# Seven half-block products in place of eight in a linear-attention and gated feed-forward kernel

## The chip, the cores and the metric

The kernel runs on one core of a Trainium2 chip. The metric is the time of one execution in microseconds (us), the median over several runs. A core has five engines, each with its own queue of instructions that it takes in order: TensorE (PE, matrix products into PSUM), VectorE (DVE), ScalarE (ACT), GpSimd (POOL) and SyncE (SP, which here only issues DMAs; POOL and ACT issue some too). PE's weight loads are shown apart, as PEld. An engine that needs another's result waits at that instruction, and all that is queued behind it waits too.

## The reference

Batch 8, 8 heads, 576 positions, head width 64; 4608 tokens of width 512; hidden width 1024.

```python
phi = lambda x: np.where(x > 0, x, np.exp(x) - 1.0) + 1.0
kv  = einsum('bhsd,bhse->bhde', phi(k), v);  z = sum(phi(k), axis=2)
num = einsum('bhsd,bhde->bhse', phi(q), kv)
den = einsum('bhsd,bhd->bhs', phi(q), z)[..., None] + 1e-06
x   = (num / den), as 4608 rows of 512
out = ((x @ w1) * (x @ w2)) @ w3 @ w_out
```

Inputs and output are float32; matrix products take bfloat16.

## The kernel before

The 576 positions of a batch are cut into 512 "main" rows (four tiles of 128) and a tail of 64. Two batches give nine tiles of 128 tokens (four, four, and one of both tails), and all 36 tiles are nine chunks of 512 tokens. The program has five kinds of work:

- The folded output weight (`w3_tr`, `wf_mm`): w3 is transposed on PE and multiplied with w_out, so that only one product follows the gates.
- phi (`phi_exp`, `phi_min`, `phi_max`): ACT takes exp to bfloat16; DVE takes min(exp, 1) in place, and then max(x + 1, that) head by head in one instruction of 256 elements with the float32 input (L162).
- Attention: `kv_half` makes phi(k)^T v with a column of ones beside v (so that z comes along), from the two 64-row halves of PE, added by ACT and DVE. A transpose DMA (`qt_load`) or PE (`q_tr`) turns phi(q). `nat_units` multiplies it with kv in half-height products of 65 columns for one or two tiles and divides on DVE: add, reciprocal, product (L271 to L275). `xt_load` or `xt_tr` turns the result to `xt`, channels by tokens. Batch 0 goes by its own path (`first_kvz`, `first_nd`).
- Gates (`f_unit`): for each of eight blocks of 128 hidden columns, four products of 512 columns for a (w1) and four for b (w2); ACT copies a out of PSUM (L376), DVE multiplies it with b to bfloat16 `ab` (L377).
- Output (`o_unit`, `o_store`): eight products of 512 columns for each tile of tokens, one eviction (L393), one store.

The order is written by hand in the string `ORDER`: each word is one unit, and the engines' queues are filled in the order of the words. A letter names the unit, the first number the batch or chunk, and a plus another engine for the copy or the queue. `GATES` holds some loads back until others have landed. What decides besides is the number of buffers: PSUM has four banks of `mm` for gates and output and two buffers of two banks, `at`, for attention; SBUF has five buffers for loaded halves and wholes of q, k and v (`ld`).

```python
def f_unit(c, f):
    a_ps, b_ps = f_open(c, f)
    for ps, w in ((a_ps, w1_sb), (b_ps, w2_sb)):
        for kc in range(KC):
            f_mm(c, f, ps, w, kc)
    f_close(c, f, a_ps, b_ps)
```

Of the kernel before, what the change touches and what calls it, by code (L numbers as in the profile page):

```python
# [14 lines left out]
NCH = 512  # L15


@with_exitstack
def kernel(
# [14 lines left out]
    NTOK = B * S  # L34
# [7 lines left out]
    n_chunks = NTOK // NCH  # L42

    tile_of, order = {}, []
    for b in range(0, B, 2):
        for key in [("J", b, j) for j in range(NJ)] + [("J", b + 1, j) for j in range(NJ)] + [("R", b, 0)]:
            tile_of[key] = len(order)
            order.append(key)  # L50
        tile_of["R", b + 1, 0] = tile_of["R", b, 0]
    NT = len(order)
# [3 lines left out]
    ld = ctx.enter_context(tc.tile_pool(name="ld", bufs=5))  # L56
    ldr = ctx.enter_context(tc.tile_pool(name="ldr", bufs=8))
    setup = ctx.enter_context(tc.tile_pool(name="setup", bufs=2))
# [3 lines left out]
    lr = ctx.enter_context(tc.tile_pool(name="lr", bufs=2))  # L62
    ab_p = ctx.enter_context(tc.tile_pool(name="ab", bufs=2))
    sm = ctx.enter_context(tc.tile_pool(name="sm", bufs=3))
    mm_ps = ctx.enter_context(tc.tile_pool(name="mm_ps", bufs=4, space=bass.MemoryType.PSUM))
    at_ps = ctx.enter_context(tc.tile_pool(name="at_ps", bufs=2, space=bass.MemoryType.PSUM))


    ident = consts.tile([P, P], BF16)
    mask = consts.tile([P, 2, 2, D], BF16)  # L70
    eps = consts.tile([P, 1], F32)
    zero = consts.tile([P, NCH], BF16)

    w1_sb = wpool.tile([P, KC, DFF], BF16)
    w2_sb = wpool.tile([P, KC, DFF], BF16)
    wo_sb = wpool.tile([P, FC, DM], BF16)
    wf_sb = wpool.tile([P, FC, DM], BF16)
    xt = wpool.tile([P, NT, KC, P], BF16)
    vt = wpool.tile([P, NJ, H, D + 1], BF16)
    vr = wpool.tile([P, H // 2, D + 1], BF16)  # L80

    def constants(part):
        if part == 0:
            make_identity(nc, ident)
        elif part == 1:

            nc.gpsimd.memset(mask, 0.0)
            nc.gpsimd.memset(mask[0:D, :, 0, :], 1.0)
            nc.gpsimd.memset(mask[D:P, :, 1, :], 1.0)
            nc.gpsimd.memset(eps, 1e-6)  # L90
            nc.gpsimd.memset(vt[:, :, :, D:D + 1], 1.0)
            nc.gpsimd.memset(vr[:, :, D:D + 1], 1.0)
        else:
            nc.vector.memset(zero, 0.0)

    def warm_up(n):

        ps = mm_ps.tile([P, NCH], F32, tag="mm", name="warm")
        for _ in range(n):
            nc.tensor.matmul(ps, zero[:, 0:P], zero, start=True, stop=True)  # L100


    raw = {}

    def load_qkv(name, src, b, part, alt=False):


        if part == 3:
            t = raw[name + "r", b] = ldr.tile([P, RW], F32, tag="ldr", name=f"{name}32r")
            for hh in range(2):  # L110
                (nc.gpsimd if alt else nc.sync).dma_start(  # L111
                    out=t[hh * R:(hh + 1) * R].rearrange("p (h d) -> p h d", d=D),
                    in_=src[b, hh * 4:(hh + 1) * 4, NJ * P:S, :].rearrange("h p d -> p h d"))
            return None
        if (name, b) not in raw:
            raw[name, b] = ld.tile([P, JW], F32, tag="ld", name=f"{name}32")
        t = raw[name, b]
        h0, h1 = ((0, 4), (4, 8), (0, 8))[part]
        W = NJ * D
        return nc.sync.dma_start(  # L120
            out=t[:, h0 * W:h1 * W].rearrange("p (h x) -> p h x", x=W),
            in_=src[b, h0:h1, 0:NJ * P, :].rearrange("h (p j) d -> p h (j d)", j=NJ))


    ph = {}

    es = {}

    def phi_exp(name, b, g):

        if g == 2:
            x, e = raw[name + "r", b], e_p.tile([P, RW], BF16, tag="er", name="er")
        else:
            x = raw[name, b][:, g * (JW // 2):(g + 1) * (JW // 2)]
            e = e_p.tile([P, JW // 2], BF16, tag="e", name="e", bufs=4)
        es[name, b, g] = x, e
        nc.scalar.activation(out=e, in_=x, func=AF.Exp)  # L137

    def phi_min(name, b, g):
        e = es[name, b, g][1]  # L140
        nc.vector.tensor_scalar_min(out=e, in0=e, scalar1=1.0)  # L141

    def phi_max(name, b, hp):

        if (name, b) not in ph:
            ph[name, b] = [None, None]
        if hp == KC:
            dr = ph[name, b][1] = phi_p.tile([P, RW], BF16, tag=name + "r", name=name + "r", bufs=3)
            todo = [(dr, *es[name, b, 2])]
        else:  # L150
            if hp == 0:
                ph[name, b][0] = phi_p.tile([P, KC, NJ, 2, D], BF16, tag=name + "j", name=name + "j")
            dj = ph[name, b][0]
            x, e = es[name, b, hp // 2]
            W = NJ * D
            todo = []
            for u in range(2):
                h = 2 * (hp % 2) + u
                todo.append((dj[:, hp, :, u, :], *(t[:, h * W:(h + 1) * W].rearrange(
                    "p (j d) -> p j d", d=D) for t in (x, e))))  # L160
        for out, x, e in todo:
            nc.vector.scalar_tensor_tensor(  # L162
                out=out, in0=x, scalar=1.0, in1=e, op0=ALU.add, op1=ALU.max)

    def copy_of(alt):
        return nc.vector.tensor_copy if alt else nc.scalar.copy

    def v_unit(b, i, alt=False):

        if i < 2:  # L170
            copy_of(alt)(  # L171
                out=vt[:, :, 4 * i:4 * i + 4, 0:D],
                in_=raw["v", b].rearrange("p (h j d) -> p j h d", h=H, j=NJ)[
                    :, :, 4 * i:4 * i + 4])
        else:
            copy_of(alt)(out=vr[:, :, 0:D], in_=raw["vr", b].rearrange("p (h d) -> p h d", d=D))


    kvs, qts, xns = {}, {}, {}

    def kv_half(b, g):


        kj, kr = ph["k", b]
        if g == 0:
            kvs[b] = att.tile([P, KC, 2, D + 1], BF16, tag="kv", name="kv")
        kvp = at_ps.tile([P, 2, 512], F32, tag="at", name="kvp")
        W = 2 * (D + 1)
        for i in range(2):
            hp = 2 * g + i  # L190
            steps = [(kj[:, hp, j].rearrange("p u d -> p (u d)"),
                      vt[:, j, 2 * hp:2 * hp + 2, :].rearrange("p h e -> p (h e)"), (0, 1))
                     for j in range(NJ)]
            steps.append((kr[:, i * P:(i + 1) * P],
                          vr[:, 2 * i:2 * i + 2, :].rearrange("p h e -> p (h e)"), (g,)))
            for n, (kk, vv, halves) in enumerate(steps):
                for r in halves:
                    rows = slice(r * R, (r + 1) * R)
                    nc.tensor.matmul(  # L199
                        kvp[:, r, i * W:(i + 1) * W], kk[rows], vv[rows],  # L200
                        start=(n == 0), stop=(n == (NJ if r == g else NJ - 1)))
        kvf = lr.tile([P, 2 * W], F32, tag="kvf", name="kvf")
        nc.scalar.copy(out=kvf, in_=kvp[:, 0, 0:2 * W])  # L203
        nc.vector.tensor_tensor(
            out=kvs[b][:, 2 * g:2 * g + 2].rearrange("p a u e -> p (a u e)"), in0=kvf,
            in1=kvp[:, 1, 0:2 * W], op=ALU.add)

    def kv_full(b, g):

        kj, kr = ph["k", b]  # L210
        if g == 0:
            kvs[b] = att.tile([P, KC, 2, D + 1], BF16, tag="kv", name="kv")
        kvp = at_ps.tile([P, 2, 512], F32, tag="at", name="kvp")
        W = 2 * (D + 1)
        rows = slice(g * R, (g + 1) * R)
        for i in range(2):
            hp = 2 * g + i
            for j in range(NJ):
                nc.tensor.matmul(kvp[:, 0, i * W:(i + 1) * W],
                                 kj[:, hp, j].rearrange("p u d -> p (u d)"),  # L220
                                 vt[:, j, 2 * hp:2 * hp + 2, :].rearrange("p h e -> p (h e)"),
                                 start=(j == 0), stop=False)
            nc.tensor.matmul(kvp[:, 0, i * W:(i + 1) * W], kr[rows, i * P:(i + 1) * P],
                             vr[rows, 2 * i:2 * i + 2, :].rearrange("p h e -> p (h e)"),
                             start=False, stop=True)
        return kvp[:, 0, 0:2 * W]

    def kv_copy(b, g, p, alt=False):
        copy_of(alt)(out=kvs[b][:, 2 * g:2 * g + 2].rearrange("p a u e -> p (a u e)"), in_=p)

# [400 lines left out]
```

## Time and profile before

| | us |
|---|---|
| median of three runs (260.99 to 262.19) | 261.28 |
| span of the profiled execution | 258.1 |
| PE busy | 237.4 |
| DVE busy | 167.9 |
| ACT busy | 129.0 |
| POOL busy | 21.1 |
| PE, gate products a and b (L371) | 75.1 and 74.9 |
| PE, output products (L390) | 63.2 |
| ACT, waits of the copy of a (L376) for PE | 55.6 |

The profile is of one execution. Busy time is the union of an engine's instructions, so that two that overlap count once. Matmuls overlap: each has a duration of 380 ns at 512 columns, but the next starts earlier. The span runs from the first to the last instruction; the rest of a run's time lies around it. A group's line in the profile names the source line, the engine, the tiles, shapes and types, how often it occurs, then its busy time and the mean duration, then the idle time before it and what ended that.

### The profile page before, as it was taken

What the parts mean: (1) busy time and instruction counts of PE and PEld (TensorE: products, weight loads), DVE (VectorE), ACT (ScalarE), POOL (GpSimd) and SP (SyncE); (2) the same over time, 40 slices, a digit from 0 to 9 for tenths busy, and PEclk for the clock granted to TensorE, in tenths of its full rate; (3) what the DMA queues carried; (4) which work ended last, traced back from release to release, by engine and by line L of the source; (5) the groups of instructions that cost most, each with busy time, mean ns of one, the idle gap of its engine ahead of it and who ended that gap; (6) DMA issues with size and microseconds to landing.
All of it is one profiled execution on the core that took longest, in us unless ns stands there. A gap on an engine that the chain in (4) does not pass through costs nothing.

```text
span 258.1 us, 4507 instructions
## 1 busy us (share of the span) xinstructions
PE 237.4 (92%) x1656; PEld 116.2 (45%) x1673; DVE 167.9 (65%) x426; ACT 129.0 (50%) x205; POOL 21.1 (8%) x42
## 2 busy tenths in 40 slices
PE   1138999999999999999999999999999999999994
PEld 1124554545454454455444444444444444444442
DVE  0025787969978979997968589468866543423320
ACT  2048587858478664677353645726533203331421
POOL 8000765000101000000000000000000000000000
PEclk9999999999999999999999999999999999999999
DMA  6999999999898599939988975934980124003024
GB/s 100 200 257 378 316 229 245 208 334 307 302 291 250 87 340 215 307 104 253 211 193 245 369 160 123 248 99 131 218 220 26 34 57 124 0 37 125 3 82 163
DMA packets 70085, 48.98 MB, mean 190 GB/s; under 512 B 34416, under 2 KB 64368, under 8 KB 70064
## 3 DMA queue, kind: packets, MB, share of 16 engines
q1 hardware_dynamic: 63104, 42.54, 61.4%
q0 software_dynamic: 6816, 6.03, 14.1%
q8 instruction: 13, 0.21, 0.3%
q10 hardware_dynamic: 144, 0.13, 0.1%
q14 instruction: 8, 0.07, 0.1%
HBM read 38.80 MB, written 9.44 MB: 187 GB/s over the span
## 4 chain that ended last, share of the span: by engine, by line
PE 84%; DMA 8%; ACT 2%; SPq 1%; issue 1%; DVE 1%; DVEq 0%; POOLq 0%
PE a_ps L371 25%; PE b_ps L371 24%; PE o_ps L390 23%; DMA k<-in_k_dram 4%; DMA w3b<-in_moe_w_dram 4%; PE kvp L199 3%; PE wf_ps L464 3%; PE nd L265 3%; SPq L111 1%; PE tp L309 1%; PE w3p L454 1%; PE xtp L285 1%; PE o_ps L417 1%; DVE qj L162 1%; ACT e L137 0%
## 5 line engine op out<-in xcount | busy, mean ns | idle before, releaser
L371 PEld LDWEIGHTS <-w_sb 128*128 128x128 bf16 x576 | 54.2, 98 | 63.4 <-issue 0.5
L377 DVE TENSOR_TENSOR ab<-a_sb,b_ps 128x512 bf16<-128x512 f32 x72 | 49.0, 684 | 46.6 <-PE b_ps L371 35.4
L371 PE MATMUL a_ps<-xt,w_sb 128*128 128x512 bf16 x288 | 75.1, 380 | 0.1
L371 PE MATMUL b_ps<-xt,w_sb 128*128 128x512 bf16 x288 | 74.9, 379 | 0.0
L376 ACT COPY a_sb<-a_ps 128x512 f32<-128x512 f32 x72 | 41.9, 586 | 56.8 <-PE a_ps L371 55.6
L390 PE MATMUL o_ps<-wf_sb,ab 128*128 128x512 bf16 x266 | 63.2, 379 | 0.7
L390 PEld LDWEIGHTS <-ab 128*128 128x128 bf16 x280 | 26.7, 98 | 30.8
L393 ACT COPY o_sb<-o_ps 128x512 f32<-128x512 f32 x24 | 14.0, 583 | 30.7 <-PE o_ps L390 30.7
L162 DVE SCALAR_TENSOR_TENSOR kj<-k,e 128x256 bf16<-128x256 f32 x64 | 23.6, 417 | 0.1
L162 DVE SCALAR_TENSOR_TENSOR qj<-q,e 128x256 bf16<-128x256 f32 x64 | 23.4, 417 | 0.1
L141 DVE TENSOR_SCALAR e<-e 128x1024 bf16<-128x1024 bf16 x32 | 13.4, 420 | 14.2 <-ACT e L137 14.2
L137 ACT ACTIVATE e<-q 128x1024 bf16<-128x1024 f32 x16 | 16.7, 1058 | 9.3 <-DMA q<-in_q_dram 9.1
L454 PE MATMUL w3p<-ident,w3b 128*128 128x128 bf16 x64 | 6.1, 253 | 15.0 <-ACT w3t L455 8.0
L137 ACT ACTIVATE e<-k 128x1024 bf16<-128x1024 f32 x16 | 16.9, 1056 | 4.1 <-DMA k<-in_k_dram 2.7
L275 DVE TENSOR_TENSOR xn<-nd,r 128x512 bf16<-128x512 f32 x28 | 18.0, 686 | 0.0
L464 PE MATMUL wf_ps<-wo_sb,w3t 128*128 128x512 bf16 x61 | 16.7, 412 | 1.0 <-ACT w3t L455 0.8
L454 PEld LDWEIGHTS <-w3b 128*128 128x128 bf16 x64 | 4.9, 113 | 16.6 <-DMA w3b<-in_moe_w_dram 8.2
L393 DVE COPY o_sb<-o_ps 128x512 f32<-128x512 f32 x11 | 7.6, 688 | 6.4 <-PE o_ps L390 6.4
L171 ACT CAST vt<-v 128x1024 bf16<-128x1024 f32 x9 | 9.3, 1046 | 2.0 <-DMA v<-in_v_dram 2.0
L203 ACT COPY kvf<-kvp 128x260 f32<-128x260 f32 x14 | 5.3, 375 | 8.9 <-PE kvp L199 8.7
L464 PEld LDWEIGHTS <-w3t 128*128 128x128 bf16 x64 | 6.2, 104 | 7.8 <-issue 1.7
L199 PE MATMUL kvp<-vt,kj 64*128 64x130 bf16 x224 | 9.2, 217 | 0.0
(81 smaller groups left out, 163.5 us busy)
## 6 DMA issues: line engine op xcount, KB each, us to landing
out_dram<-o_sb SPq DMA_DIRECT2D x31, 256.0 KB, 3.2
k<-in_k_dram SPq DMA_DIRECT2D x7, 1024.0 KB, 8.6
q<-in_q_dram SPq DMA_DIRECT2D x7, 1024.0 KB, 8.2
v<-in_v_dram SPq DMA_DIRECT2D x6, 1024.0 KB, 7.4
w3b<-in_moe_w_dram POOLq DMA_DIRECT2D x8, 256.0 KB, 7.1
v<-in_v_dram SPq DMA_DIRECT2D x4, 512.0 KB, 8.5
w_sb<-in_moe_w_dram POOLq DMA_DIRECT2D x8, 256.0 KB, 11.3
out_dram<-o_sb SPq DMA_DIRECT2D x9, 128.0 KB, 2.4
```

The costliest lines, as they stand in the source:

```text
L137: nc.scalar.activation(out=e, in_=x, func=AF.Exp)
L141: nc.vector.tensor_scalar_min(out=e, in0=e, scalar1=1.0)
L162: nc.vector.scalar_tensor_tensor(out=out, in0=x, scalar=1.0, in1=e, op0=ALU.add, op1=ALU.max)
L199: nc.tensor.matmul(kvp[:, r, i * W:(i + 1) * W], kk[rows], vv[rows], start=(n == 0), stop=(n == (NJ if r == g else NJ - 1)))
L275: nc.vector.tensor_tensor(out=dst.rearrange("p (c u) e -> p u c e", u=2), in0=v4[:, :, :, 0:D], in1=r[0:n].unsqueeze(3).to_broadcast([n, 2 ...
L371: nc.tensor.matmul(ps, w[:, kc, f * P:(f + 1) * P], xt[:, 4 * c:4 * c + 4, kc, :], start=(kc == 0), stop=(kc == KC - 1))
L376: nc.scalar.copy(out=a_sb, in_=a_ps)
L377: nc.vector.tensor_mul(out=abs_[c][:, f, :], in0=a_sb, in1=b_ps)
L390: nc.tensor.matmul(o_ps, ab[:, f, m * P:(m + 1) * P], wf_sb[:, f, :], start=(f == 0), stop=(f == FC - 1))
L393: copy_of(alt)(out=o_sb, in_=o_ps)
L454: nc.tensor.transpose(tp[:, kc, :], raw["w3", i][:, kc * P:(kc + 1) * P], ident)
L464: nc.tensor.matmul(wfs[i], w3ts[i][:, kc, :], wo_sb[:, kc, :], start=(kc == 0), stop=(kc == FC - 1))
```

## The change

The arithmetic of the gates and the output is done in half blocks by a form of Strassen's scheme, which needs seven products of half blocks where the plain way needs eight, at the price of sums and differences of blocks before and after.

- Chunks: chunk c below 8 is now batch c's main rows, and chunk 8 holds the eight tails (`xtr`).
- Gates: for chunks 1 to 8 and the pairs of hidden blocks (0,4), (1,5), (2,6) the new `g_unit` makes seven units in place of two `f_unit`s, each of four products of 256 columns. They take differences of weight blocks (`ws_make`, once) and of x blocks (`xs_make`, four for each chunk). The results are combined through snapshots: ACT copies a bank out, DVE adds the snapshot to another bank, and `g_mul` multiplies a with b out of SBUF, on DVE or POOL. Blocks 3 and 7 and all of chunk 0 keep `f_unit`.
- Output: for chunks 0 to 7 `w_unit` makes seven units of eight products of 256 columns in place of four `o_unit`s of eight of 512, with differences of `ab` (`s_make`) and of the folded weight (`wt_make`). Chunk 8 keeps the plain way. One store now holds two tiles.
- Attention: `kv_full` and `nat` use PE's whole height for every batch, the first with a tail padded with zeros, the second against a kv block with zeros beside the diagonal; `nat` takes one tile at a time. Batch 0 has no path of its own, and the warm-up products are gone.
- phi: DVE or POOL takes max(x, 0) + 1 to bfloat16 (`phi_max1`), DVE then the minimum with exp, both in bfloat16 (`phi_min`).
- Buffers: loads come in halves (eight buffers of half the size); w3 is staged in `ab`'s buffers; `at` has one buffer of two banks; two banks `o` and `u` serve transposes, Strassen's running sums and output.
- `ORDER` and `GATES` are new throughout; `copy_of` can name POOL as a third engine.

The core of the diff:

```diff
+    def phi_max1(name, b, g, alt):
+        x, w, r = part_of(name, b, g)
+        y = es["y", name, b, g] = e_p.tile([P, w], BF16, tag="y" + r, name="y" + r, bufs=2)
+        (nc.gpsimd if alt else nc.vector).tensor_scalar(
+            out=y, in0=x, scalar1=0.0, scalar2=1.0, op0=ALU.max, op1=ALU.add)
...
+        for c in range(2):
+            nc.vector.tensor_tensor(out=p[0][:, 2 * g + c].rearrange("p j u d -> p u j d"),
+                                    in0=e[:, c], in1=y[:, c], op=ALU.min)
...
+    def nat(b, j):
+        nd = at_ps.tile([P, 2, NCH], F32, tag="at", name="nd")
...
+        for hp in range(KC):
+            g, i = divmod(hp, 2)
...
+            nc.tensor.matmul(nd[0:n, g, i * 2 * E1:(i + 1) * 2 * E1], w,
+                             kvs[b % 2][:, i, g].rearrange("p u e -> p (u e)"), start=True, stop=True)
...
+    def xs_make(c, i, alt):
...
+        a, b = ((lambda: blk(0, 1), lambda: blk(0, 0)), (lambda: blk(1, 1), lambda: s[:, 0]),
+                (lambda: blk(1, 1), lambda: blk(0, 1)), (lambda: blk(1, 0), lambda: s[:, 1]))[i]
+        (nc.gpsimd if alt else nc.vector).tensor_tensor(
+            out=s[:, i], in0=a(), in1=b(), op=ALU.subtract)
...
+    def g_product(t, c, q, a, m, first):
+        for w in range(2):
+            for k in range(2):
...
+                nc.tensor.matmul(t[:, w], l, r, start=(first and w == 0 and k == 0), stop=(k == 1),
+                                 skip_group_check=True)
...
+    def g_unit(c, q, i):
...
+        a, m, name, first = ((), ((0, 0, 0), (0, 0, 0), "u", True), ((0, 0, 1), (0, 1, 0), "t", True),
+                             ((1, 1), (1, 1), "u", False), ((1, 0), (1, 0), "t2", True),
+                             ((1, 2), (1, 2), "u", False), ((1, 3), (0, 1, 1), "t2", False),
+                             ((0, 1, 1), (1, 3), "u", False))[i]
+        if first:
+            pool, tag = (o_ps_p, "ou"[q % 2]) if name == "u" else (mm_ps, "mm")
+            st[name] = pool.tile([P, 2, HN], F32, tag=tag, name="g" + name)
+        t = st[name]
+        g_product(t, c, q, a, m, first)
+        if i in (1, 3, 4):
+            s = st["s", i] = fsm("gs")
+            nc.scalar.copy(out=s, in_=t)
+        elif i in (2, 5, 6):
+            s = st["c", i] = fsm("gc")
+            nc.vector.tensor_tensor(out=s, in0=st["s", {2: 1, 5: 4, 6: 3}[i]], in1=t, op=ALU.add)
+        else:
+            s = fsm("ga")
+            nc.scalar.copy(out=s[:, 0], in_=t[:, 0])
+            nc.vector.tensor_mul(out=abs_[c][:, q + 4, 0:HN], in0=s[:, 0], in1=t[:, 1])
+
+    def g_mul(c, q, i, alt):
+        s = cs_[c, q]["c", i]
+        f, r = {2: (q, 0), 5: (q + 4, 1), 6: (q, 1)}[i]
+        (nc.gpsimd if alt else nc.vector).tensor_mul(
+            out=abs_[c][:, f, r * HN:(r + 1) * HN], in0=s[:, 0], in1=s[:, 1])
...
+    def product(t, a, w, first):
+        for qd in range(2):
+            for f in range(FC // 2):
+                nc.tensor.matmul(t[:, qd], a[:, f, qd * P:(qd + 1) * P], w[:, f, :],
+                                 start=(first and qd == 0 and f == 0), stop=(f == FC // 2 - 1),
+                                 skip_group_check=True)
...
+    def w_unit(c, i):
+        s = sts.get(c)
+        if i == 1:
+            product(bank(c, "u"), a_block(c, 0, 0), w_block(0, 0), True)
+            snap(c, "p1", banks[c, "u"])
+        elif i == 2:
+            product(bank(c, "t"), a_block(c, 0, 1), w_block(1, 0), True)
+            nc.vector.tensor_tensor(out=rows_of(c, 0)[:, :, 0:HN], in0=snaps[c, "p1"],
+                                    in1=banks[c, "t"], op=ALU.add)
...
```

In the new order `F`, `h` and `i` are plain gate units, `G` and `m` Strassen's gate units and their products, `e` and `d` the differences of weights and x, `V` and `s` the output units and their differences, `K` and `A` kv and `nat`, `x`/`X`, `y`/`Y` and `z`/`Z` the three steps of phi for k and q, `T` and `D` the transpose DMAs, `L`, `M`, `N` and `R` the loads. The head of the new order up to the first gates of chunk 0, and a piece from its middle:

```diff
+    R0.0+ L0.0+ N0.0 L0.1 E1 M0.0 y0.2 R0.1+ M0.1 X0.0 M1.0+ y0.0 I1 I0 E2 Y0.0 v0.0+ x0.2 C1
...
+    T0.1 A1.4 x2.0 h0 d1.2+ N2.0 d1.0 d1.1+ y2.0 t3 z2.0 N2.1 h1 h2 h3 i0 i1 M3.0 e1.2 Y2.1
...
+    Z5.1 D2.1 G3.2.2 G3.2.5 m3.1.6+ G3.2.6 A4.4 D4.0 x6.0 m3.2.2+ z6.0 G3.1.7 m3.2.5+ F3.3 T5.0
```

## The prediction

> **What bounds the kernel now.** I read the table of slices first, then busy time by stage, the chain of waits, and the groups kept apart by shape. In the slices a digit is the busy tenth of 6.45 us.
>
> ```profile
> PE   1138999999999999999999999999999999999994
> DVE  0025787969978979997968589468866543423320
> DMA  6999999999898599939988975934980124003024
> ```
>
> The reader is to see two regions: a head in which TensorE (PE) waits, and a long stretch in which it never does. The stages, cut where the gates of chunk 0 begin to run without a break (start and end, length, then busy time and instructions of each engine, granted clock, DMA share, GB/s):
>
> ```profile
> 49.60:60.00 10.40, 10.40 (x89) 5.22 (x89) 8.29 (x23) 7.29 (x13) 0.00 (x0) 1.00 1.24 290
> 60.00:120.00 60.00, 59.79 (x481) 30.05 (x485) 54.68 (x148) 39.45 (x65) 2.45 (x4) 1.00 0.90 241
> 120.00:190.00 70.00, 69.67 (x493) 32.27 (x494) 54.76 (x149) 35.64 (x59) 0.00 (x0) 1.00 0.81 201
> 190.00:254.40 64.40, 64.16 (x367) 30.13 (x369) 25.07 (x47) 18.30 (x32) 0.00 (x0) 1.00 0.26 77
> ```
>
> PE is busy for 204.0 of 204.8 us at a granted clock of 1.00. VectorE (DVE) is the next engine, 54.7 of 60 us in the second row. GpSimd (POOL) has nothing to do. Busy time includes the tails of pipelined matmuls, so the real price is the step from one to the next. The chain of waits and the groups by shape show it (chain: start, length; group: busy us, mean ns of one, idle before):
>
> ```profile
> 55.82 0.86 PE a_ps L371 x4
> ...
> 131.82 1.73 PE o_ps L390 x8
> ```
>
> ```profile
> L417 PE MATMUL o_ps<-wf_sb,ab 128*128 128x256 bf16 x16 | 1.9, 272 | 0.0
> ```
>
> A 512-column matmul steps 0.86/4 = 0.216 us. The 16 of 256 columns lie in 1.91 us on the timeline, so (1.91 - 0.27)/15 = 0.109: half the columns, half the price. Priced so, PE's work after 49.6 us is 560 x 0.216 for gates, 62.2 for the output and 17.3 for attention, 200.5 us in 204.8. The list loses 2.1%.
>
> **Prices.** Steps are starts apart on the timeline where one follows another; they are a little under the durations in these groups.
>
> ```profile
> L377 DVE TENSOR_TENSOR ab<-a_sb,b_ps 128x512 bf16<-128x512 f32 x72 | 49.0, 684 | 46.6 <-PE b_ps L371 35.4 <-ACT a_sb L376 8.0 <-ACT er L137 2.2
> L162 DVE SCALAR_TENSOR_TENSOR kj<-k,e 128x256 bf16<-128x256 f32 x64 | 23.6, 417 | 0.1
> L286 DVE COPY xt<-xtp 128x512 bf16<-128x512 bf16 x3 | 1.2, 416 | 0.0
> L171 DVE CAST vt<-v 128x1024 bf16<-128x1024 f32 x7 | 4.8, 702 | 0.0
> L176 DVE CAST vr<-v32r 128x256 bf16<-128x256 f32 x3 | 1.0, 339 | 0.0
> L87 POOL MEMSET mask<- 128x256 bf16 x1 | 0.4, 360 | 0.0
> masks.py:199 POOL TENSOR_SCALAR_AFFINE_SELECT ident<-ident 128x128 bf16<-128x128 bf16 x1 | 0.3, 287 | 0.1
> ```
>
> DVE: 512 elements with a float32 operand from PSUM step 0.60, 256 step 0.34; a cast of 1024 steps 0.63; a normalised tile of attention (add, reciprocal, product) takes 1.02 alone and 0.87 in a pair. PE: a 130-column full-height matmul (L219) and a 128-column transpose step 0.056.
>
> **The change, part by part.**
>
> *PE.* Gates: 576 x 0.216 = 124.4 become 192 x 0.216 + 672 x 0.109 = 114.7, so -9.7. Output: 62.2 becomes 448 x 0.109 + 24 x 0.216 + 16 x 0.109 = 55.7, so -6.5. Batch 0 loses its numerator and denominator products (-1.9), half of the q transposes (32 x 0.056 = -1.8) and the warm-up (9 x 0.216 = -1.9). Full-height kv is 16 x 0.056 + 2 x 0.11 = 1.12 per batch against 1.13 for 36 half-height ones: nothing, but -0.6 with batch 0. The numerators are 20 x 0.056 = 1.12 per batch, eight times, against 40 x 0.022 seven times: +2.8. The sum is -19.6, to 209.4.
>
> *DVE.* The gate products fall from 72 to 24, but 72 sums of a snapshot with PSUM (0.60), 24 products (0.34) and 17 of the 72 SBUF products (0.34) come: 43.2 to 71.6. Output: 11 copies (6.9) become 24 sums (15.3). Attention: 40 single tiles (40.8) in place of 28 paired and 7 single (31.5). Block differences: 15 of 1024, 4 of the folded weight, 10 of 512, 2 of 768. No row has a two-input operation with all operands bfloat16 in SBUF, and phi's new minimum (64 of 512, 8 more) is one too. Lower bound: two elements a cycle as the bfloat16 copy L286, 0.335 for 512 and 0.60 for 1024. Upper: one a cycle as L377, 0.60 and 1.13. The nearest row has bfloat16 on both sides, so I take the lower and keep both. Phi is then 30 x 0.63 + 72 x 0.335 + 1.4 = 44.4 against 61.4 (upper: 63.5). DVE's whole sum is 195.4 (upper 228.0).
>
> The Trainium skill, "VectorE: DVE Perf Modes", section on the tier table, gives a two-input operation twice the rate when all is bfloat16 in SBUF; the sum by it is the lower one, and no run here shows it.
>
> *POOL.* It gets 55 products of 256, 22 differences of 512, 17 of 1024, 6 of 768 and a few of phi. Lower bound: the memset's slope, (360 - 223)/128 = 1.07 ns an element (the 128-column memset of ident took 223). Upper: two inputs at twice the select's slope, 2 x (287 - 86)/128 = 3.1. I take the middle, 2.1, plus 0.1 each: 140 us with the DMA issues, 77 to 180 by the ends; it stays below PE's sum.
>
> *ScalarE* (ACT): 72 snapshots, 24 half copies and 32 output evictions replace 96 whole ones. It has 145.9 us, 119 of them beside PE's 179: hidden. Its cover is PE; with a late ACT copy the next Strassen product on that bank is late.
>
> *The stages.* I split the written order at `h0` (first gates of chunk 0) and at `A7.4` (end of attention). From `h0` to `A7.4` PE has 143.5, DVE 138.8 (upper 162.3), POOL 96; behind it PE has 35.5 and DVE 23.0. So in the first stage DVE lies within 4% of PE, and it has a new neighbour. The one row in which DVE ran beside POOL is the cast L176: 291 ns twice, and 437 at 38.0 us, while POOL issued a weight load. In this stage 106 DVE instructions read SBUF through two inputs or at the fast rate, and POOL is busy 96/143.5 = 67% of it. With 0.147 us for each that meets POOL: 106 x 0.67 x 0.147 = 10.4. DVE then sets the stage: 149.2. Its ends are nothing (PE's 143.5) and a wait for whole POOL instructions, which is the third rival.
>
> The Trainium skill, "SBUF — State Buffer", section "Who interferes with whom", speaks against this change: DVE and GpSimd share a port pair, and the second to come is blocked for the other's whole instruction. The casts L171, 0.72 and 0.76 us beside POOL's DMA issues against a median of 0.69, don't show so much. By that rule the sum would be the third rival's.
>
> *Waits and queues.* Each new sum on DVE waits for a PE product and an ACT snapshot. Behind it in DVE's queue stand phi and the attention tiles of later batches, and for those wait SP's transposes (28 for 24, 4.8 us to land), with the next loads queued behind on SP. Kv and numerators now share one PSUM buffer instead of two, 1.02 of DVE between; this is hidden as long as gates stand between them on PE. The larger stores (16 of 512 KB for 32 of 256) cost no time before the end.
>
> *The head.* The order puts batch 1's loads, both batches' attention and three gate units before `h0`: 13.6 MB must land, against 12.1 in 49.6 us before (3.84 in 20 us, 6.02 in the next 20, some 2.2 after). At the 0.28 MB/us of 20 to 50 us, 1.5 MB more are 5.4 us. But PE's part of the head holds 5.2 us of gates that no longer stand behind it, already out of the 143.5, and DVE (33.6) and ACT (26.9) fit. Ends: 49.6 (as before) and 57; I take 53.
>
> *Sum.* 53 + 149.2 + 35.5 + 3.8 (2.1% of 179) + 3.7 (last matmul to the end, 258.1 - 254.4) = 245.2, where the profiled execution's span is 258.1. The median of the runs, 261.3, is 3.2 above the span: **248 us**.
>
> **Rivals.**
>
> *Nothing in the way:* PE sets both stages, head as before: 49.6 + 143.5 + 35.5 + 3.8 + 3.7 + 3.2 = 239. For: the list of before lost 2.1% beside a DVE that was 91% busy. Against: DVE now leaves it 4% in place of 9%.
>
> *Bfloat16 pairs at one a cycle:* DVE sets the stage with 162.3: 53 + 162.3 + 35.5 + 3.8 + 3.7 + 3.2 = 261, no change. For: every two-input row here runs so. Against: each has a float32 operand.
>
> *DVE and POOL block each other:* a DVE instruction that meets POOL waits half a mean POOL instruction, 1.09/2: 106 x 0.67 x 0.545 = 38.7 more on DVE, 177.5 for the stage, **277 us, slower**. It decides from 23.3 us of such waits (261.3 - 3.2 - 53 - 35.5 - 3.8 - 3.7 - 138.8), 0.22 for each of the 106. For: L176. Against: its size there was 0.147.
>
> *DMA:* before batch 7's kv some 29.6 MB must pass in 112 us, 0.26 a us. The row of 60 to 120 us had 0.241, which costs 11 us in place of the 5.7 that DVE costs: 254. Against: after 50 us no engine waited long on a load.
>
> **How the numbers follow.** Forecast 0.52; nothing in the way 0.14; one a cycle 0.06; blocking in full or in good part 0.21; DMA 0.07. I call a change below 0.5% (1.3 us; the runs lie 1.2 apart) none. Half of the one-a-cycle case falls to no change and half to slower, with a little of the forecast's edge too: faster 0.70, none 0.05, slower 0.25. The range is 238, a little under the first rival, to 268, part of the way into blocking; for the likeliest case alone 240 to 254.
>
> **What would show it.** Right: half-width gate products stepping 0.11 with `h0` near 53 us; phi's minimum near 0.42 each; DVE over 90% busy until attention ends and PE losing a few per cent there, none behind. Wrong: minima at 0.68; DVE instructions stretched to the length of POOL's beside them; loads named before phi's exponentials. A head beyond 60 us would break the sum by itself.

## The result, and the profile after

The changed kernel takes 280.5 us (median of four runs, 280.25 to 280.92), where the kernel before took 261.1 beside it: a ratio of 1.073, 95% interval 1.070 to 1.077. It is slower; the prediction said faster. The profiled execution has a span of 278.4 us.

The slices of the changed kernel, each 6.96 us long, show where:

```profile
PE   0047999688677987796789969986898999999993
DVE  0295774899999999999999999999999999888770
POOL 7565936379385679557866895587366245247120
DMA  7999899998579999999998795840192070210305
```

Before, PE had a row of nines from the fifth slice to the last but one, and DVE wavered below it. Now DVE has the unbroken row of nines, from slice 9 to slice 34, and PE wavers. The stages, cut at `h0` (57.5), `A7.4` (236.9) and the last matmul (273.7), in the columns of the prediction's table by stage:

```profile
57.50:100.00 42.50, 33.94 (x254) 23.26 (x253) 42.09 (x71) 27.24 (x46) 30.25 (x20) 0.96 0.87 209
100.00:140.00 40.00, 31.27 (x267) 23.83 (x267) 39.52 (x67) 26.72 (x46) 29.62 (x23) 1.00 1.02 261
140.00:190.00 50.00, 46.73 (x383) 35.81 (x384) 49.23 (x92) 33.27 (x57) 36.68 (x29) 0.93 0.75 203
190.00:236.90 46.90, 42.75 (x374) 34.05 (x371) 45.05 (x86) 21.04 (x40) 23.90 (x21) 1.00 0.33 85
236.90:273.70 36.80, 36.38 (x290) 27.93 (x288) 28.04 (x49) 15.78 (x31) 13.46 (x13) 1.00 0.22 76
```

In the stage from `h0` to `A7.4`, 179.4 us long, DVE (third pair) is busy for 175.9, and PE, whose matmuls at one step after another come to 143.4, loses 36.0. Part of this isn't waiting: the granted clock, 1.00 in every row of before, is 0.96 and 0.93 in two of these, and 0.04 x 42.5 + 0.07 x 50 is 5.2 us of PE's work at the full clock. What lowers the clock was not tried. Behind `A7.4` PE is full again. The groups of the changed kernel, by shape:

```profile
L190 DVE TENSOR_TENSOR kj<-e,y 128x512 bf16<-128x512 bf16 x32 | 24.8, 817 | 0.0
L190 DVE TENSOR_TENSOR qj<-e,y 128x512 bf16<-128x512 bf16 x32 | 23.2, 765 | 0.3
L388 DVE TENSOR_TENSOR gc<-gs,gt 128x512 f32<-128x512 f32 x48 | 32.1, 678 | 2.7 <-PE gt L364 2.1 <-ACT gs L385 0.5
L173 DVE TENSOR_SCALAR y<-q 128x1024 bf16<-128x1024 f32 x14 | 14.9, 1068 | 2.7 <-DMA q<-in_q_dram 2.7
L397 POOL TENSOR_TENSOR ab<-gc 128x256 bf16<-128x256 f32 x55 | 42.9, 789 | 58.6 <-DVE gc L388 47.1 <-DVE r L272 10.2 <-PE a_ps L310 1.0
L411 POOL TENSOR_TENSOR s<-ab 128x1024 bf16<-128x1024 bf16 x6 | 13.6, 2264 | 3.0 <-DVE ab L316 2.9
```

Phi's minimum (L190) has a shortest duration of 406 ns, as forecast, and a mean of 765 to 817. The sum L388 has the same type of operation, but takes one of its inputs from PSUM: its mean is 678, and no instruction of it is long. The stretched ones are those that read SBUF through both inputs or run at the fast rate, which is that of `y`: 1024 elements in 0.68 us undisturbed, where L388 takes as long for 512. The timeline shows what lies beside them, first DVE, then POOL (start, length):

```profile
100.45 1.95 DVE L173 TENSOR_SCALAR y<-q 128x1024 bf16<-128x1024 f32 x1
...
109.30 2.79 DVE L190 TENSOR_TENSOR qj<-e,y 128x512 bf16<-128x512 bf16 x2
```

```profile
99.67 2.17 POOL L411 TENSOR_TENSOR s<-ab 128x1024 bf16<-128x1024 bf16 x1 [1.02 <-DVE ab L316]
...
108.82 2.12 POOL L411 TENSOR_TENSOR s<-ab,s 128x1024 bf16<-128x1024 bf16 x1
110.91 0.90 POOL L397 TENSOR_TENSOR ab<-gc 128x256 bf16<-128x256 f32 x1
```

A `y` takes 0.68 us where POOL is quiet; this one begins at 100.45 and ends at 102.40, 0.56 after POOL's difference that began before it (101.84). Two minima should take 0.84 together; these take 2.79. They end at 111.22 and 112.09, each 0.28 after the POOL instruction beside it (110.94 and 111.81).

To add this up, I take each DVE instruction's duration less the usual one of its shape (the tenth percentile in the same run), and call the sum the *stretch*. It is 44.3 us in the changed kernel, 39.0 of it between `h0` and `A7.4`, and practically all in instructions that overlap one of POOL's; before the change it was 3.5. Of the 46 minima in that stage 41 meet a POOL instruction, and these hold 22.8 us: 0.56 for each that meets one. That mean hides two kinds. Twenty minima keep their 0.41 us, though most of them overlap a POOL instruction too; 26 take 0.67 to 2.34, and 24 of these end 0.28 or 0.29 us after the end of a POOL instruction that began before them, as the two above. (The other two began beside one of POOL's own `y`.) The eight `y` of the stage that take over 0.8 us each end 0.55 or 0.56 after one. So a blocked instruction stands still until POOL's is done, and its price is about what is left of that.

This is still read from one run. Two theories were set against each other: A, POOL's instructions block DVE's, and that sets the time; and D, the new order with its queues, buffers and transfers would lose the time without any blocking.

### The profile page after: what moved, and what is told of

Read it like the earlier page. It is cut to its first block, busy times and chain, and to the rows that moved or that the text cites. A ratio compares the mean times of both kernels' runs of the same rounds, so it can differ in the third digit from the quotient of the medians.

```text
span 278.4 us, 5153 instructions
## 1 busy us (share of the span) xinstructions
PE 227.3 (82%) x1848; PEld 167.8 (60%) x1848; DVE 237.5 (85%) x434; ACT 152.8 (55%) x256; POOL 169.1 (61%) x159
## 3 DMA queue, kind: packets, MB, share of 16 engines
q1 hardware_dynamic: 65008, 41.56, 56.7%
## 4 chain that ended last, share of the span: by engine, by line
PE 38%; DVE 26%; DMA 19%; issue 7%; POOL 6%; ACT 2%; SPq 2%; DVEq 0%; ACTq 0%; POOLq 0%
PE gu L364 10%; DMA q<-in_q_dram 9%; PE gt L364 8%; DMA w3b<-in_moe_w_dram 6%; PE u L423 5%; DVE kj L190 5%; PE t L423 4%; DVE qj L190 4%; DVE gc L388 3%; POOL xs L349 3%; DVE y L173 3%; PE b_ps L310 3%; DVE ab L316 3%; PE a_ps L310 3%; DMA xt<-xn 2%
## 5 line engine op out<-in xcount | busy, mean ns | idle before, releaser
L397 POOL TENSOR_TENSOR ab<-gc 128x256 bf16<-128x256 f32 x55 | 42.9, 789 | 58.6 <-DVE gc L388 47.1
L364 PEld LDWEIGHTS <-ws 128*128 128x128 bf16 x384 | 37.5, 99 | 7.7 <-issue 1.1
L385 ACT COPY gs<-gu 128x512 f32<-128x512 f32 x48 | 27.6, 590 | 20.5 <-PE gu L364 20.3
L388 DVE TENSOR_TENSOR gc<-gs,gt 128x512 f32<-128x512 f32 x48 | 32.1, 678 | 2.7 <-PE gt L364 2.1
L423 PEld LDWEIGHTS <-s 128*128 128x128 bf16 x256 | 25.4, 101 | 9.5 <-POOL s L411 3.1
L364 PE MATMUL gu<-xs,ws 128*128 128x256 bf16 x192 | 28.2, 279 | 1.3 <-DVE xs L349 0.9
L310 PE MATMUL a_ps<-xt,w_sb 128*128 128x512 bf16 x88 | 24.5, 391 | 1.7 <-DVE ab L316 1.1
L310 PE MATMUL b_ps<-xt,w_sb 128*128 128x512 bf16 x88 | 24.2, 387 | 1.2 <-DVE ab L316 1.2
L190 DVE TENSOR_TENSOR kj<-e,y 128x512 bf16<-128x512 bf16 x32 | 24.8, 817 | 0.0
L190 DVE TENSOR_TENSOR qj<-e,y 128x512 bf16<-128x512 bf16 x32 | 23.2, 765 | 0.3
L315 ACT COPY a_sb<-a_ps 128x512 f32<-128x512 f32 x24 | 13.8, 585 | 14.3 <-PE a_ps L310 11.5
```

The lines of the kernel that those rows point to most:

```text
L190: nc.vector.tensor_tensor(out=p[0][:, 2 * g + c].rearrange("p j u d -> p u j d"), in0=e[:, c], in1=y[:, c], op=ALU.min)
L310: nc.tensor.matmul(ps, w[:, kc, f * P:(f + 1) * P], xt_of(c)[:, :, kc, :], start=(kc == 0), stop=(kc == KC - 1))
L364: nc.tensor.matmul(t[:, w], l, r, start=(first and w == 0 and k == 0), stop=(k == 1), skip_group_check=True)
L385: nc.scalar.copy(out=s, in_=t)
L388: nc.vector.tensor_tensor(out=s, in0=st["s", {2: 1, 5: 4, 6: 3}[i]], in1=t, op=ALU.add)
L397: (nc.gpsimd if alt else nc.vector).tensor_mul(out=abs_[c][:, f, r * HN:(r + 1) * HN], in0=s[:, 0], in1=s[:, 1])
```

## The experiments

**POOL's work on DVE (e1).** Every plus is taken off the words `m`, `d`, `s`, `e` and `y`, so that DVE does all of POOL's arithmetic (`y` stands for `Y` too). A piece of the order:

```diff
-    G2.2.2 V1.7 m2.0.6+ v4.0 V1.6 y4.2+ A3.2 N4.1 G2.1.1 y4.0 G2.1.2 m2.2.2+ N5.1
+    G2.2.2 V1.7 m2.0.6 v4.0 V1.6 y4.2 A3.2 N4.1 G2.1.1 y4.0 G2.1.2 m2.2.2 N5.1
```

> All of POOL's products, differences and maxima go to DVE; POOL only issues DMAs. Theory A (the two engines block each other): DVE's own work grows by some 42 us to 237, of it 174 between the first gates of chunk 0 and the end of attention, but its two-input instructions lose their stretch of 44 us, the minima step back to 0.42 each: about 274 us, so that POOL's help was worth next to nothing. Rival B (DVE's long instructions come from something else, and POOL's help is real): 174 + 41 for that stage, about 315 us.

281.2 us, ratio 1.077 (1.069 to 1.085): 7 above theory A's 274, far from rival B's 315. The groups of this kernel:

```profile
L190 DVE TENSOR_TENSOR qj<-e,y 128x512 bf16<-128x512 bf16 x32 | 12.1, 418 | 0.3
L190 DVE TENSOR_TENSOR kj<-e,y 128x512 bf16<-128x512 bf16 x32 | 12.0, 417 | 0.0
```

With POOL quiet the minima are 418 and 417 ns; the stretch is 3.3. But DVE is busy for 238.2 us, and was for 237.5. The work that POOL took from DVE is worth 238.2 - 3.3 less 237.5 - 44.3, that is 41.7 us; its price in stretch was 44.3 - 3.3 = 41.0. The help was worth nothing, as the two times say as well.

**POOL writes but doesn't read (e2).** POOL's operations become memsets of the same tiles; the differences, products and parts of phi that POOL made are left out.

```diff
-        (nc.gpsimd if alt else nc.vector).tensor_mul(
+        if alt:
+            nc.gpsimd.memset(abs_[c][:, f, r * HN:(r + 1) * HN], 0.01)
+            return
+        nc.vector.tensor_mul(
```

> Every product, difference and maximum that POOL makes becomes a POOL memset of the same output, so that part of the computation is left out and POOL writes without reading. Theory A (DVE's second input waits for POOL's reads): minima back to 0.42 in nearly all cases, DVE 139 us and PE 144 in the stage up to the end of attention, about 247 us. Rival B (DVE's own sum and the order of its queue hold the time): still above 272 us.

268.6 us, neither theory A's 247 nor rival B's 272 and more. Its runs lie far apart (264.2 to 273.6), so I use only its groups, with lines shifted by three, and the durations of `y` (shortest/median/longest in ns, first and last start):

```profile
L176 DVE TENSOR_SCALAR y<-q 128x1024 bf16<-128x1024 f32 x14 | 20.0, 1428 | 0.2 <-DMA q<-in_q_dram 0.2
...
L193 DVE TENSOR_TENSOR qj<-e,y 128x512 bf16<-128x512 bf16 x32 | 12.1, 419 | 0.7 <-DMA qt<-qj 0.4
```

```profile
L176 DVE TENSOR_SCALAR y<-q x14: 675/686/6450, 13.4 to 178.5; 128x1024 bf16<-128x1024 f32 x14
```

The minima have their usual duration beside POOL's memsets: ten of the 64 meet one, and the longest takes 426 ns. `y`, one input at the fast rate, is stretched by 10.5 us in sum, but not evenly: most have their usual 0.68, and five, of 0.83 to 6.45 us, stand beside memsets that follow each other without a break and end 0.54 or 0.55 us after one of them. So two kinds of blocking are at work: of the second input, by POOL's reads; and of the fast rate, by its writes too, as long as these go on.

The Trainium skill, "SBUF — State Buffer", section "Who interferes with whom", says just this: DVE's second input and its two-port modes go through a port pair shared with GpSimd, the first against GpSimd's reads only. The prediction had this rule beside a row of 0.147 us; the run agrees with the rule.

**Phi's x + 1 on ACT (e4).** The question is whether less DVE work at the fast rate helps.

```diff
-        (nc.gpsimd if alt else nc.vector).tensor_scalar(
-            out=y, in0=x, scalar1=0.0, scalar2=1.0, op0=ALU.max, op1=ALU.add)
+        nc.scalar.activation(out=y, in_=x, func=AF.Identity, bias=one[:, 0:1])
+        nc.vector.tensor_scalar_min(out=es[name, b, g], in0=es[name, b, g], scalar1=1.0)
```

> x + 1 comes from ACT in bfloat16, DVE takes min(exp, 1) in place and the maximum of both; POOL keeps its products and differences. DVE's own work falls by 9 us, but as many of its instructions read through two inputs or at the fast rate. Theory A: the stretch stays at about 40 us, 268 to 274 us in all. Rival B: the casts L173 were what was slow, the stretch goes with them, below 262 us.

287.1 us in one run; the stretch is 44.7 as before, and ACT is busy for 188.6 us. `h0` comes at 61.7. The stretch is theory A's; the time is 13 us beyond its range. Other instructions took the stretch over; the run tells no more.

**POOL's long work gone (e5).** POOL's differences are replaced by one constant tile that nothing has to make, its products become memsets, its parts of phi go to DVE. What POOL computed is left out.

```diff
-        (nc.gpsimd if alt else nc.vector).tensor_tensor(out=s[i], in0=a(), in1=b(), op=op)
+        if alt:
+            s[i] = flat4
+            return
+        nc.vector.tensor_tensor(out=s[i], in0=a(), in1=b(), op=op)
```

> POOL's part of the changed kernel taken away almost whole: its differences (of weights, of x, of the gates' product) are left out and a constant tile is read in their place, its 46 products before the end of attention become memsets of 256 elements, phi's maxima go to DVE. That part of the computation is left out. Theory A (blocking is all of the loss): DVE has 141 us and PE 143.5 between the first gates of chunk 0 and the end of attention, the stage takes at most 150, the kernel about 250. Rival D (the order holds PE and DVE so close together that some 15 us are lost there whatever POOL does): the stage takes 158 or more, the kernel 260 or more.

265.2 us, ratio 1.015 (1.011 to 1.018); the stretch is 4.6, and the stage 167.0 us. So 12.4 us of it go with POOL's long work. Theory A's 250 is missed, and rival D's 260 or more came. PE still loses 23.6 us, with DVE busy for only 143.6 of 167.0. Theory A doesn't explain those: something else stands behind DVE. e9 shows what.

**POOL added to the kernel before (e6).** One POOL addition per gate unit, of two tiles of 512 that are there anyway, into a tile that nobody reads any more.

```diff
         f_close(c, f, a_ps, b_ps)
+        nc.gpsimd.tensor_tensor(out=zero, in0=abs_[c][:, f, :], in1=abs_[c][:, f, :], op=ALU.add)
```

> The kernel before, plus one POOL addition behind each plain gate unit: it reads the bfloat16 tile just written (512 elements) and writes to a tile that nobody reads. Nothing waits for it. Theory A (blocking): 64 or so additions of 1.2 to 1.5 us stretch DVE's two-input and fast instructions beside them, by some 0.4 us each, 20 to 40 us more on DVE, which had 5 of 60 us free: 270 to 285 us. Rival B (no blocking between the two): 261 us, as before.

270.3 us, ratio 1.036 (1.032 to 1.040), at the lower edge of theory A's range. The groups:

```profile
L385 POOL TENSOR_TENSOR zero<-ab 128x512 bf16<-128x512 bf16 x70 | 74.9, 1070 | 136.1 <-DVE ab L377 119.1 <-DVE r L271 14.4 <-DVE er L141 2.0
L377 DVE TENSOR_TENSOR ab<-a_sb,b_ps 128x512 bf16<-128x512 f32 x72 | 48.7, 681 | 39.2 <-PE b_ps L371 30.3 <-ACT a_sb L376 7.5 <-ACT er L137 1.2
L162 DVE SCALAR_TENSOR_TENSOR kj<-k,e 128x256 bf16<-128x256 f32 x64 | 31.5, 536 | 0.1
```

L162, two inputs from SBUF, goes from 417 to 536 ns in the mean; L377, one input from PSUM, stays (684 and 681). The stretch rises from 3.5 to 20.4 us, and the time by 9, in a kernel whose DVE had a little room (54.7 of 60 us busy in its fullest stage). This shows the blocking by adding it alone.

**Plain gates, Strassen's output only (e3).** All gates by `f_unit`; POOL has no arithmetic. A piece of the order:

```diff
-    G1.0.1 F0.4 X2.1 Z2.1 T2.0 y2.2 e1.0+ v2.2 e1.1+ d1.3+ y2.1 F0.2
+    F1.0 F0.4 X2.1 Z2.1 T2.0 y2.2 v2.2 y2.1 F0.2
```

> Strassen for the output alone, plain gates in every chunk, nothing but DMA issues on POOL. By theory A DVE has 127.5 us in the stage up to the end of attention against PE's 151, and nothing stretches it: PE sets the time, 57 + 155 + 38 + 6 = 256 us, below the kernel before. By a rival C (the new order, the head or the single attention buffer cost the time, whatever POOL does) it stays above 265 us.

274.0 us, ratio 1.047 (1.042 to 1.052). DVE has only 131.2 us of work in a stage of 172.4, the stretch is 2.5, and PE, with 151.0 us of work there, loses 21.4. By theory A alone PE would have set the stage; rival C's number came. So there is a second loss with neither blocking nor a full DVE, as in e5. Its cause was not tried here: PE sits idle for 11.3 us up to 160, at transfers' shares of 0.96 to 1.11, and for another 4.3 behind that, at shares of 0.55 and less, which full transfers don't explain.

**Strassen's output in the kernel before (e7, e8).** `w_unit`, `s_make` and `wt_make` are set into the old kernel, as one block of seven units per chunk with the differences on DVE: in e7 for chunks 0 to 7, in e8 for 4 to 7 only. To make room, four buffers stand for the copies of a and the snapshots, and two for output rows. A piece of the order, before and in e7:

```diff
-    L4.3 N3.2 M4.3 O0.3 Y3.1 A2.1 F1.7 z3.1 S0.0 N4.3 S0.1 Z3.0
+    L4.3 N3.2 M4.3 Y3.1 A2.1 F1.7 s1.1 s1.2 z3.1 N4.3 Z3.0 s1.0 s1.3
```

> The kernel before, with the seven products for the output of chunks 0 to 7 alone, in one block of PE work for each chunk, block differences on DVE, nothing on POOL. PE has 6.5 us less; DVE has 8.4 us more for sums and 19 more for differences. If the half-block products cost what they should (0.109 us) and DVE's room is what matters: between 60 and 120 us DVE goes from 54.7 to some 62 of 60 us, and the end comes at 257 to 263 us. If the running sums in one bank hold PE up between the products: above 266 us.

> As the run with the output's seven products in the kernel before, but for chunks 4 to 7 alone, where DVE has room (25 of 64 us busy behind 190 us). PE has 4 x 0.82 = 3.3 us less. If DVE's room decides: 258 to 259 us, faster than both kernels by 1%. If the running sums hold PE up: 262 us or more.

293.2 us (ratio 1.123, 1.118 to 1.127) and 272.9 (1.044, 1.041 to 1.047). PE idles 27.9 and 10.4 us after 50 us where it had 0.8 before; in e8, 6.1 of it is one wait of a running sum for the snapshot of the same bank, in e7 6.7 are three such waits. Both came out on the second side of their expectation, where the running sums hold PE up, and far beyond it. So seven products laid one behind the other do stall on their own snapshots; that this is most of the loss is shown for e8 alone. It says nothing of the new order, which spreads them; and since buffers were cut too, no more is read from these two.

**Transfers (e9 to e12).** In e5 the transfers' share stands near one as long as PE loses time. The windows of e5, and then of e9, in the columns of the table by stage:

```profile
60.00:100.00 40.00, 33.56 (x274) 24.75 (x272) 33.37 (x72) 27.57 (x48) 2.33 (x9) 0.96 1.04 225
100.00:140.00 40.00, 34.72 (x317) 28.08 (x316) 34.55 (x80) 29.22 (x49) 4.95 (x17) 1.00 1.06 282
140.00:160.00 20.00, 15.49 (x123) 11.01 (x121) 15.25 (x35) 12.99 (x20) 0.00 (x0) 1.00 1.01 253
160.00:200.00 40.00, 40.00 (x353) 32.33 (x351) 37.47 (x84) 25.61 (x47) 3.83 (x13) 0.96 0.58 145
```

```profile
60.00:100.00 40.00, 39.16 (x344) 30.38 (x343) 39.26 (x91) 33.74 (x59) 2.92 (x12) 1.00 1.10 293
100.00:140.00 40.00, 39.49 (x341) 30.31 (x339) 39.45 (x89) 33.55 (x55) 4.20 (x15) 1.00 1.00 315
```

In e5 PE is idle for 16 us from 60 to 160, at shares of 1.01 to 1.06, and never from 160 to 200, at 0.58. This says when, not why. e9 makes the transposing DMAs of e5 plain ones between the same tiles: 12 of 512 KB (the expectation's "20 large" is a miscount) and 8 of 64 KB.

```diff
-        nc.sync.dma_start(out=dst, in_=s, transpose=True)
+        nc.sync.dma_start(out=dst, in_=s)
```

> The kernel of e5 (POOL's large work gone, 265.2 us, PE 23.5 us short of its 143.5 in the stage from h0 to A7.4) with the 20 large transposing DMAs (T, and D of parts 0) and the 8 small ones of q's tails made plain copies of the same bytes between the same tiles; the transposition is left out, and the dependences stay. Eight small ones of the tails' x stay transposing. The transfers' share of 16 DMA engines in e5 is 0.95 to 1.14 in every 20 us from 60 to 160, where PE loses 17 us. Theory D1 (the transfers are at their capacity, and the transposing ones take much of it): the loss falls by 8 us or more, 250 to 257 us. Theory D2 (the order and the in-order queues of DVE and ACT lose the time, the DMAs only look busy): 263 to 267 us.

e10 leaves out the stores of six chunks, e11 does both, and e12 does both in the changed kernel with all its POOL work.

```diff
     def o_store(c, r, half=None):
+        if c < 6:
+            return
         o_sb = o_sbs[c, r]
```

> The kernel of e5 without the stores of chunks 0 to 5 (12 of 512 KB, 6.3 MB; that part of the output is not written). It takes away bytes, and also the places in SP's queue where a store waits for a sum of DVE with the next loads behind it. D1 (transfers or SP's queue hold PE up): 6.3 MB at the 0.26 MB/us of e5 are 24 us of transfers, so most of the 17 us go: 247 to 255 us. D2 (order, DVE and ACT): 262 to 266 us.

> Both edits, plain copies and no stores of chunks 0 to 5, in the kernel of e5. D1: stage near PE's own 143.5 to 150 and head 55: 243 to 251 us. D2: above 260 us.

> The same two edits in the changed kernel itself, with POOL's work as it is. Theory A (DVE, stretched beside POOL to 177 us in the stage, sets its length, and it was 98 to 99% busy there): no more than 4 us gained, 276 to 281 us. If transfers alone set the stage: 258 to 266 us.

| | median us | ratio to before, 95% | stage `h0` to `A7.4` | PE's loss in it |
|---|---|---|---|---|
| after | 280.5 | 1.070 to 1.077 | 179.4 | 36.0 |
| e12: after, plain DMAs, no stores | 280.0 | 1.066 to 1.077 | 180.9 | 37.5 |
| e5: POOL light | 265.2 | 1.011 to 1.018 | 167.0 | 23.6 |
| e10: POOL light, no stores | 256.4 | 0.979 to 0.986 | 154.5 | 11.1 |
| e9: POOL light, plain DMAs | 249.8 | 0.948 to 0.960 | 147.6 | 4.2 |
| e11: POOL light, both | 248.5 | 0.947 to 0.958 | 148.3 | 4.9 |

e9 is 0.2 us below D1's range and e10 1.4 us above it; e11 is within D1's, e12 within theory A's. D2, that the order loses the time by itself, is false: the same order, with the same queues and buffers, loses 4.2 us. The clock has a part in the difference of e5 and e9: 0.96 in two of e5's rows is 0.04 x 80 = 3.2 us of PE's work, and e9 has 1.00, so that about 16 of the 19.4 us belong to the transposing DMAs. e9's first window moves 293 GB/s where e5's moves 225, at much the same share. The queue's lines, of e5 and of e9 (packets, MB, share of 16 engines' span):

```profile
q1 hardware_dynamic: 65008, 41.56, 61.9%
```

```profile
q1 hardware_dynamic: 40624, 41.56, 56.4%
```

The same 41.56 MB take 0.619 x 263.9 = 163.4 us with the transpositions and 0.564 x 245.5 = 138.5 without: 24.9 us of all 16 engines. But e9 frees SP too. The issue of a large transposing DMA holds SP's queue, with the next loads behind it, for up to 7.2 us, a plain one for 0.6 at most (e5, then e9, durations as above):

```profile
L248 SPq DMA_TRANSPOSE qt<-qj x6: 1983/2980/7216, 62.7 to 187.8; - x6
```

```profile
L248 SPq DMA_DIRECT2D qt<-qj x6: 514/530/600, 63.7 to 168.2; - x6
```

The 12 large ones hold SP for 37.6 us in e5 and 6.3 in e9. e10, which keeps them but takes 6.3 MB away, gives 12.5 us in the stage; its profile has a clock of 1.00 and is of its fastest run (252.8 us), so about 9 of these are the stores' own, as in the medians (265.2 and 256.4). Taking away either the transpositions or other bytes gives PE time back, so it is room in the transfers that counts, or in SP's queue, which lost its stores in e10; no run here tells these two apart. e12 shows the order of the two causes: with DVE stretched, the transfers' room is worth nothing that can be measured. No version here beats the kernel before: those of the table that are faster than it leave out a part of the computation or of the output.

## Why the prediction was wrong

The forecast's case was that DVE sets the stage at 149.2 us. DVE did set it, at 179.4; the failed step is a term of the sum, "106 x 0.67 x 0.147 = 10.4", DVE's interplay with POOL. It measured 39.0, and these 28.6 us turn the forecast of 248, faster, into 276, slower. The other terms, each as forecast and as measured:

| term | forecast | measured |
|---|---|---|
| head to `h0` | 53 | 57.5 |
| PE's own work, `h0` to `A7.4` | 143.5 | 143.4 |
| DVE's own work there | 138.8 | 175.9 - 39.0 = 136.9 |
| blocking by POOL | 10.4 | 39.0 |
| other stalls (forecast for both stages, measured in the first) | 3.8 | 179.4 - 175.9 = 3.5 |
| behind `A7.4` to the last matmul | 35.5 | 36.8 |
| to the end of the span | 3.7 | 278.4 - 273.7 = 4.7 |
| median less span | 3.2 | 2.1 |

The measured column, with 136.9 for DVE's own work, adds up to 280.5.

- *The size came from the wrong row.* The cast L176, 0.147 us longer, stood beside a DMA issue of 0.74 us; what came were POOL instructions of 0.8 to 2.3 us that read two tiles. The third rival, 0.545 for each that meets one, came out at 0.56 for the minima; its 38.7 us for the stage were 39.0, and its 277 us were 280.5. It had a chance of 0.21. That it came so near is in part luck: it took half a POOL instruction of 1.09 us for two in three, and measured were a mean of 1.37 us, minima that met POOL in 41 of 46 cases, and 26 of these stretched. The page's rule pointed to this rival, and the row was not near enough to outweigh it.
- *Prices of work on PE and DVE were right, POOL's was too low.* Products of 256 columns step 0.109 us (eight in 0.87 to 0.88), and the minimum takes 0.41 where nothing blocks it, so "one a cycle" (0.60) is false. POOL is busy for 169.1 us, where the forecast had 140 with the DMA issues, and in the stage for 120.5 against 96; its share there is 0.67 as forecast only because the stage grew alike.
- *The DMA rival was priced too low.* It gave 11 us from bytes alone. Once blocking was gone, PE still lost 23.6 us (e5); e9 puts some 16 of them down to the transposition of the same bytes, by the 16 engines or by SP's queue, and some 3 are the clock's. In the changed kernel this lies under DVE's stretch (e12).
- *"Nothing in the way"* had PE setting the stage and 239 us. With both causes gone (e9) the stage is 147.6 and the time 249.8: the list itself loses 4.2 us, 2.8% of the stage where 2.1% were assumed, and the head comes at 56.3.
- *The head.* 57.5 is a little beyond the forecast's 49.6 to 57. From 20 to 60 us the transfers moved 254 and 218 GB/s, where 280 were assumed. The kernels with little or no POOL arithmetic have `h0` at 55.1 to 56.3, but so has e12 (56.3), with all of it. What slowed the transfers there was not tried.

## What to carry to other kernels

Work given to POOL is not free for DVE: count the DVE instructions that read SBUF twice or run at the fast rate, and charge each that meets a POOL instruction with a good part of that instruction's length (here 0.56 us in the mean, and 2 us where a long one had just begun), before counting what was taken off DVE. Sums with one operand in PSUM pay nothing. And when a limit is lifted, look at once for the next one under it: here each of two causes alone looked as though it were the only one, and removing only the lower one changed nothing.

## What the runs showed of the hardware

- A DVE instruction with one SBUF input that can run at the fast rate (`y`) is stretched even by POOL's memsets, up to 6.45 us for 0.68 beside an unbroken run of them (e2); a two-input minimum is not (419 ns).
- What POOL blocks resumes when POOL's instruction is done: 24 of the 26 stretched minima of the stage end 0.28 or 0.29 us after it, the eight long `y` 0.55 or 0.56. A sum with one operand in PSUM is not blocked (longest 689 ns, mean 678).
- A transposing DMA costs far more than its bytes: with 20 of them, 6.8 MB, the queue took 24.9 us more of all 16 engines than with plain copies of the same size, and 65,008 packets against 40,624. Its issue holds SP's queue as well: 3.0 us in the median for 512 KB of `qt` in e5, against 0.53.
- POOL's time per element differs by form, at the shortest: 2.1 ns for the two-input bfloat16 difference of 1024 (2118 ns), 2.8 for the product of two float32 tiles of 256 (715 ns), 3.5 for `y`, one float32 input of 1024 (3624 ns).
